# Second half's K transform in front of two rows of the first inverse, two tiles for modulation weights, spectra of block 1 kept in tiles

## The chip, the cores and the metric

The kernel runs on one core of one Trainium2 chip. The core has five engines with an instruction stream each: PE (matmuls), DVE (vector), ACT (activations), POOL and SP. Here POOL does little arithmetic and issues one queue of DMA transfers, SP issues another. The metric is the device time of one execution in microseconds, as the median of several runs. The profile shows one further execution, whose own time is given beside its span.

## The reference

The input is a sequence u of 2048 tokens with 576 channels. Six vectors sa, ca, ga, sb, cb, gb of 576 numbers come from a condition vector c. A state-space layer (S4D, 128 states per channel) is a long causal convolution along the sequence, one kernel K per channel; behind it stands a feed-forward layer (FFN).

```python
P = exp((A * dt)[:, :, None] * arange(2048))        # A, C, dt from the inputs
K = 2 * einsum("dn,dnl->dl", C, P).real             # 576 kernels of 2048 taps
y = irfft(rfft(K, 4096) * rfft(u, 4096))[:2048]     # causal convolution
A_ref(u) = y + u * D_skip

mod = (silu(c) @ w_mod).reshape(1, 6, 576)          # sa, ca, ga, sb, cb, gb
h = layernorm(x) * (1 + ca) + sa
x = x + ga * A_ref(h)
h = layernorm(x) * (1 + cb) + sb
x = x + gb * (relu(h @ w1) @ w2)                    # 576 -> 4608 -> 576
```

## The kernel before, in words

**Blocks and halves.** The sequence is worked through in 4 blocks (s = 0 to 3) of 512 tokens, held as tiles x of 128 partitions x 4 x 576. The channels are split in two halves, p = 0 and 1, of 288. A block's convolution is done by the discrete Fourier transform of 1024 points, whose larger factor is a matmul with a constant table (fcU for the input, fcK for the kernel, gc for the way back) and whose smaller factor, of 4, is a butterfly of additions on DVE. For each half: transform of u (PE, `ps_f`, then ACT copies it to a tile Z, then DVE's butterfly gives the spectrum U), transform of the SSM kernel's block (the same, giving K; for s above 0 a second spectrum, K2, made of K and the spectrum R of the block before), the product of spectra, one term for every earlier block t (Y += Ka * Ua, with temporaries T, on DVE at line 509), a butterfly giving V, and the inverse (PE, `ps_i`, line 983, four rows n2 = 0 to 3 of the result), which DVE adds to x. The spectra that later blocks need go to DRAM: Ud[t][p], Rd[t][p] and Kd[t][p], 1152 KB each, and are loaded into tiles Ua, R and Ka when a product needs them. All spectra tiles of the later blocks come from one pool, tag "S", of 6 buffers.

**The FFN.** Each block's FFN has 36 groups of 128 hidden channels. Both of its matmuls are split in a high and a low part: `w` tiles hold the weight's high part (an ACT copy, line 1255 or 1262) and the low part (DVE's subtraction, `w<-r,w`, in pieces of 640, 64 and 512 columns); xh, xl are those of the input. A group is 14 matmuls into `hps` (line 1284; 2 PSUM buffers), ACT's relu `hh` (line 1289), DVE's remainder `hl` (line 1290), which frees the `hps` buffer, and 14 matmuls into `acc` (line 1309). The low parts are made in block 0 and kept in DRAM for the later blocks.

**Interleaving.** Block 0's convolution, `conv0`, comes ahead of the first FFN and is written out by hand. The convolution of block s + 1 runs inside the FFN of block s: it is a generator (`conv(s)`) which `step` advances twice per FFN group, by an amount set by a rate per block. The SSM kernel's generation for later blocks (`kps`, line 440 on PE, lines 408 to 414 on DVE, from tables W1d, W2d and Zd in DRAM) is interleaved in the same way. A tile scheduler then fixes the order of instructions on each engine, and every engine runs its own stream in order: an instruction that waits holds up all behind it. Tiles with a tag share a fixed number of buffers, so a new tile waits for the last reader of the one whose place it takes. POOL issues its transfers in program order as well.

**The end of `conv0`.** It works with tiles of its own, tags S0 to S3, kt, and two PSUM pools (one of 2 buffers, for the first inverse, and one of 4). In the program's order it does: the first half up to V; the second half's transform of u; x's load; the first half's inverse (`back`, rows n2 = 0, 2, 1, 3, each with the addition to x and a `bn_stats` for the second norm); the second half's butterfly U1; its K transform (`transform1`, lines 786 and 788: for each of 8 results one matmul with `early` and one with `early` or the negated table `fcKn`, then an ACT copy into WK, line 789); K1, the product Y1, V1; the second half's inverse; the norm; transposes of h (`ps_t`, line 1034); the FFN's first matmul.

**The late modulation weights** (`mod_late`). sb, cb and gb are needed for the second norm and the FFN's end. For each of them POOL loads a 576 x 576 slice of w_mod in two pieces (1152 and 144 KB, lines 596 and 597) into a tile with tag "wm", of which there is one buffer; PE multiplies it with c (`mps`, line 626, 25 instructions, each recorded in two), ACT copies the row, PE transposes it (`mpt`, lines 637 and 638) and ACT writes the vector.

## Time and profile before

| | us |
|---|---|
| median of 3 runs | 1384.04 |
| lowest, highest | 1380.11, 1387.81 |
| profiled execution, its own time | 1382.06 |
| its span (first to last instruction) | 1380.3 |
| PE busy | 1233.1 |
| DVE busy | 869.9 |
| ACT busy | 503.1 |
| first matmul of the FFN starts at | 232.61 |

The mean granted clock of PE was 0.939 of full speed. A profile row reads: start, busy time, engine, line, operation, output<-inputs, shapes; in brackets the time for which the engine stood idle just before and the instruction that released it. A line number is that of the kernel before; line 509 is a helper through which most of DVE's arithmetic goes, so such rows are told apart by their tiles' names. PEclk is the clock that the throttle granted to PE in a stretch.

### The profile page before, as it was taken

How to read it: one execution, taken by the hardware profiler on the slowest of the kernel's cores; microseconds unless marked ns; L12 is line 12 of the kernel's file. 1: busy time of each engine (PE TensorE's matmuls, PEld its weight loads, DVE VectorE, ACT ScalarE, POOL GpSimd, SP SyncE). 2: the span in 40 equal slices, each digit the busy share in tenths (PEclk: the TensorE clock that was granted, in tenths of full speed). 3: DMA queues.
4: the chain of work that ended last, by engine and by line, in shares of the span. 5: the costliest groups of instructions: out<-in, count | busy, mean ns of one | idle time of the engine just before them, and what ended most of it. 6: DMA issues, size and time to landing. Idle time of an engine off the chain costs nothing.

```text
span 1380.3 us, 26042 instructions
## 1 busy us (share of the span) xinstructions
PE 1233.1 (89%) x10608; PEld 977.5 (71%) x10608; DVE 869.9 (63%) x1351; ACT 503.1 (36%) x1014; POOL 197.9 (14%) x275
## 2 busy tenths in 40 slices
PE   5124778999999987989999999999999999999998
PEld 3123556777777766667777877777877878888886
DVE  5976977999886698559834987264999232111111
ACT  7985233222224322522234324433322253222231
POOL 1776222111121100021010010000010000000000
PEclk9555787999999999899999999999999999999999
DMA  6666399788888949598788995676998657666651
GB/s 193 240 242 239 101 331 364 271 314 306 283 317 282 334 157 337 164 353 316 238 279 304 323 369 179 204 240 210 365 323 299 202 152 212 198 198 193 205 172 60
DMA packets 134568, 347.55 MB, mean 252 GB/s; under 512 B 22448, under 2 KB 22768, under 8 KB 134448
## 3 DMA queue, kind: packets, MB, share of 16 engines
q1 hardware_dynamic: 106256, 218.36, 48.6%
q0 software_dynamic: 27904, 126.94, 25.2%
q8 instruction: 83, 1.36, 0.4%
q10 hardware_dynamic: 288, 0.59, 0.1%
q14 instruction: 37, 0.30, 0.1%
HBM read 264.44 MB, written 81.40 MB: 251 GB/s over the span
## 4 chain that ended last, share of the span: by engine, by line
PE 67%; DVE 18%; DMA 7%; issue 5%; ACT 3%; POOL 1%; SPq 0%; DVEq 0%; ACTq 0%; POOLq 0%
PE acc L1309 25%; PE hps L1284 25%; PE kps L440 5%; DVE Y L509 4%; PE ps_f L749 4%; DVE T L509 4%; PE kps L262 3%; DMA Ua<-Ud 2%; PE ps_i L983 2%; DVE W L509 2%; DMA Ud<-U 1%; DVE k L133 1%; DVE hl L1290 1%; PE kps L606 1%; DMA wm_gb<-in_w_mod_dram 1%
## 5 line engine op out<-in xcount | busy, mean ns | idle before, releaser
L1309 PE MATMUL acc<-hh,w 128*128 128x512 f32 x1296 | 424.2, 401 | 6.2 <-DVE w L509 6.1
L1284 PE MATMUL hps<-xh,w 128*128 128x512 f32 x1152 | 392.0, 400 | 0.6 <-issue 0.4
L1309 PEld LDWEIGHTS acc<-hh,w 128*128 128x128 f32 x1296 | 243.0, 189 | 60.3 <-DVE w L509 7.8
L1309 PE MATMUL acc<-hl,w 128*128 128x512 f32 x720 | 278.9, 399 | 0.0
L1290 DVE SCALAR_TENSOR_TENSOR hl<-hps,hh 128x512 fp32r<-128x512 f32 x144 | 98.7, 686 | 281.5 <-ACT hh L1289 281.4
L1284 PEld LDWEIGHTS hps<-xh,w 128*128 128x128 f32 x1152 | 214.8, 188 | 47.1 <-ACT xh L1046 1.1
L1284 PE MATMUL hps<-xl,w 128*128 128x512 f32 x576 | 229.0, 397 | 0.2 <-DVE xl L1051 0.2
L1289 ACT ACTIVATE hh<-hps 128x512 fp32r<-128x512 f32 x144 | 86.0, 597 | 336.4 <-PE hps L1284 335.9
L1262 ACT ACTIVATE w<-r 128x576 fp32r<-128x576 f32 x144 | 98.7, 686 | 219.1 <-issue 172.5
L1309 PEld LDWEIGHTS acc<-hl,w 128*128 128x128 f32 x720 | 135.3, 188 | 28.3
L1284 PEld LDWEIGHTS hps<-xl,w 128*128 128x128 f32 x576 | 108.2, 188 | 24.4 <-DVE xl L1051 1.2
L1255 ACT ACTIVATE w<-r 128x640 fp32r<-128x640 f32 x142 | 104.0, 732 | 18.7 <-DMA r<-in_w_dram 18.6
L262 PE MATMUL kps<-W,W 128*32 128x16 f32 x2304 | 40.0, 218 | 78.1 <-POOL W L59 49.7
L1284 PE MATMUL hps<-xs,w 128*128 128x512 f32 x288 | 95.5, 412 | 5.4 <-DVE hl L1290 5.4
L262 PEld LDWEIGHTS kps<-W,W 128*32 128x32 f32 x2304 | 37.6, 151 | 82.7 <-POOL W L59 51.0
L440 PEld LDWEIGHTS kps<-W1r,W2r 128*32 128x32 f32 x3456 | 69.0, 146 | 31.7 <-issue 17.6
L509 DVE TENSOR_TENSOR Y<-Y,T 128x1152 f32<-128x1152 f32 x64 | 84.9, 1349 | 0.2
L440 PE MATMUL kps<-W1r,W2r 128*32 128x48 f32 (+2 forms) x3456 | 78.3, 238 | 7.3 <-DVE W1r L412 4.2
L750 ACT ACTIVATE Z<-ps_f 128x288 f32<-128x288 f32 x104 | 42.4, 408 | 64.3 <-PE ps_f L749 63.7
L1284 PEld LDWEIGHTS hps<-xs,w 128*128 128x128 f32 x288 | 52.6, 188 | 18.3 <-DVE hl L1290 7.1
L509 DVE TENSOR_TENSOR w<-r,w 128x512 fp32r<-128x512 f32 (+2 forms) x108 | 57.9, 571 | 8.7 <-ACT w L1262 8.7
L509 DVE TENSOR_TENSOR W<-Z 128x576 f32<-128x576 f32 x52 | 37.0, 751 | 28.9 <-ACT Z L750 28.9
(214 smaller groups left out, 1381.7 us busy)
## 6 DMA issues: line engine op xcount, KB each, us to landing
r<-in_w_dram SPq DMA_DIRECT2D x144, 320.0 KB, 4.4
r<-in_w_dram SPq DMA_DIRECT2D x144, 288.0 KB, 3.8
w<-L1d SPq DMA_DIRECT2D x108, 320.0 KB, 3.0
w<-L2d SPq DMA_DIRECT2D x108, 288.0 KB, 3.2
W2r<-W2d POOLq DMA_DIRECT2D x18, 1536.0 KB, 9.3
W2d<-W SPq DMA_DIRECT2D x12, 1536.0 KB, 7.8
Ua<-Ud POOLq DMA_DIRECT2D x15, 1152.0 KB, 11.1
W<-W1d POOLq DMA_DIRECT2D x18, 768.0 KB, 8.9
```

The source lines that it names most:

```text
L262: self.nc.tensor.matmul(ps[32 * dd : 32 * dd + 32, 12 * u + q, :], W2[:, r, :, ch], W1[:, u, :, r, ch], start=(r == 0), stop=(r == 1),)
L440: nc.tensor.matmul(ps[32 * dd : 32 * dd + 32, q, :], W2[:, r, :, ch], W1[:, :na, r, ch], start=(r == 0), stop=(r == 1),)
L509: return self.kept(self.nc.vector.tensor_tensor(*args, **kw))
L749: kept(nc.tensor.matmul(o, fc[:, n2, c, :], src(n2), start=True, stop=True))
L750: nc.scalar.activation(Z[:, n2, c], ps[:, :PC], AF.Copy)
L983: self.nc.tensor.matmul(ps[:, :PC], a, b, start=(i == 0), stop=(i == len(todo) - 1))
L1255: nc.scalar.activation(w[:, 0], r, AF.Copy)
L1262: nc.scalar.activation(w[:, 0:D], r2[g], AF.Copy)
L1284: nc.tensor.matmul(ps, a, x, start=(i == 0), stop=(i == 13))
L1289: nc.scalar.activation(hh, ps, AF.Relu)
L1290: nc.vector.scalar_tensor_tensor(hl, ps, 0.0, hh, op0=ALU.max, op1=ALU.subtract)
L1309: nc.tensor.matmul(acc[i], a, x, start=(f == 0 and j in (0, 3, 6, 9, 12)), stop=(f == NF - 1 and j in (2, 5, 8, 11, 13)),)
```

## The change

It has three parts.

1. **Two buffers for the modulation weights.** The loads of sb's and cb's weights are issued one behind the other; gb's is issued when sb's product has been written, into sb's tile.
2. **The order at the end of `conv0`.** U1's butterfly comes first, then rows n2 = 0 and 2 of the first inverse with their additions to x, then the whole K transform of the second half, and behind its last matmul the matmuls of rows n2 = 1 and 3. Their additions to x and their statistics are done after V1, ahead of the second inverse. For space, the vector dsk (D_skip) and the table fcKn lie in the tiles of fcU and fcK, which are filled later. The FFN's first weight conversions are issued behind the last of cb's activations instead of the K transform's last one. W1d's and Zd's stores, which the program puts behind the last weight load issued so far, stand behind gb's.
3. **Spectra kept in tiles.** In block 1 the second term of the product (t = 1) multiplies with R, which is in a tile already, instead of loading the same numbers again as Ka. In all blocks the second half's U stays in a tile (in the pool of h, which has been read by then), so that the term t = s does not load it; in the last block it isn't stored. This takes six transfers of 1152 KB away: two Ka and one Ua in block 1, one Ua each in blocks 2 and 3, one store of U in block 3.

The core of the diff:

```diff
-        for i, nm in ((3, "sb"), (4, "cb"), (5, "gb")):
-            w = cv.tile([P, 5, D], F32, tag="wm", bufs=1, name=f"wm_{nm}")
-            d = self.wm = self.mod_weights(w, slice(i * D, (i + 1) * D), nc.gpsimd)
-            if i == 3:
-                behind(d)
+        ws = {}
+
+        def load(i, nm):
+            w = ws[nm] = cv.tile([P, 5, D], F32, tag="wm", bufs=2, name=f"wm_{nm}")
+            self.wm = self.mod_weights(w, slice(i * D, (i + 1) * D), nc.gpsimd)
+            return self.wm
+
+        behind(load(3, "sb"))
+        load(4, "cb")
+        for nm in ("sb", "cb", "gb"):
             yield
+            w = ws[nm]
...
-            if nm == "gb":
+            if nm == "sb":
+                load(5, "gb")
+            elif nm == "gb":
                 yield
...
         def spec_U(p, Z):
-            U = self.spec(f"U_{s}_{p}")
+            if p:
+                U = self.hb.tile([P, 4, 2, PC], F32, tag="h", name=f"U_{s}_{p}")
+            else:
+                U = self.spec(f"U_{s}_{p}")
...
-            if s + 1 < NB or p == 1:
+            if s + 1 < NB:
                 self.save(self.Ud[s][p], U)
-            Us.append(U if p == 0 else None)
+            Us.append(U)
...
             R = self.load(self.Rd[s - 1][p], "R")
+            Rs.append(R)
...
-                Ka = Ks[p] if t == 0 else self.load(self.Kd[s - t][p], "Ka")
-                Ua = Us[p] if (t == s and Us[p] is not None) else self.load(self.Ud[t][p], "Ua")
+                if t == 0 or s == 1:
+                    Ka = (Rs if t else Ks)[p]
+                else:
+                    Ka = self.load(self.Kd[s - t][p], "Ka")
+                Ua = Us[p] if t == s else self.load(self.Ud[t][p], "Ua")
...
-        self.dsk = cva.tile([1, D], F32, name="dsk")
+        self.dsk = self.fcU[0:1].rearrange("p a b c -> p (a b c)")[:, :D]
...
+        fcKn = self.fcK.rearrange("p a b c -> p (a b) c")[:, 0:4]
...
-        half = back(0, ops(V))
-        next(half)
         U1 = S(3, "U1")
         run(self.butterfly2(W, U1, -1))
         self.save(self.Ud[0][1], U1)
-        run(half)
+        run(back(0, ops(V), (0, 2)))
         self.cps, self.nps = cpsb, 4
         WK = S(1, "WK")
         run(self.transform1(sK1, early[:, 1], fcKn, WK))
+        self.cps, self.nps = cpsa, 2
+        odd = [back(0, ops(V), (i,)) for i in (1, 3)]
+        with tc.issue_after(self.mm1.ins):
+            for h in odd:
+                next(h)
+        self.cps, self.nps = cpsb, 4
         next(mod)
...
-        with tc.issue_after(self.end1.ins):
+        with tc.issue_after(self.mact.ins):
             next(self.start)
...
+        for h in odd:
+            run(h)
```

**PE at the end of `conv0`**, from the middle of the first inverse to the product with sb's weights (`ps_i` is an inverse's row, `ps_f` a transform, `mps_sb` the product). Before:

```order
L983 MATMUL ps_i<-V_2295,gc 128x288 x6
L983 MATMUL ps_i<-V_2295,gcn 128x288 x2
L786 MATMUL ps_f<-kt,early 128x288
L983 MATMUL ps_i<-V_2295,gc 128x288 x2
L983 MATMUL ps_i<-V_2295,gcn 128x288
L983 MATMUL ps_i<-V_2295,gc 128x288 x4
L983 MATMUL ps_i<-V_2295,gcn 128x288
L788 MATMUL ps_f<-kt,early 128x288
L786 MATMUL ps_f<-kt,early 128x288
L788 MATMUL ps_f<-kt,fcKn 128x288
```

Now (the pairs L794 and L796 go on to the eighth between the last two pieces):

```order
L998 MATMUL ps_i<-V_2293,gc 128x288 x6
L998 MATMUL ps_i<-V_2293,gcn 128x288 x2
L794 MATMUL ps_f<-kt,early 128x288
L796 MATMUL ps_f<-kt,early 128x288
L794 MATMUL ps_f<-kt,early 128x288
L796 MATMUL ps_f<-kt,fcK 128x288
```

```order
L794 MATMUL ps_f<-kt,early 128x288
L796 MATMUL ps_f<-kt,fcK 128x288
L998 MATMUL ps_i<-V_2293,gc 128x288 x2
L998 MATMUL ps_i<-V_2293,gcn 128x288
L998 MATMUL ps_i<-V_2293,gc 128x288 x4
L998 MATMUL ps_i<-V_2293,gcn 128x288
L632 MATMUL mps_sb<-wm_sb,cb 32x128 x20
```

The eight matmuls of rows 1 and 3 have moved from behind the K transform's first matmul to behind its last.

**POOL's transfers in the same stretch**: weights, the second half's U and K on their way to DRAM (Ud_1, Rd_1), the kernel generator's tables (Zd, W1d). Before:

```order
L596 DMA wm_sb<-in_w_mod_dram 128x4x576
L740 DMA Ud_1_102<-U_2562 128x4x576
L596 DMA wm_cb<-in_w_mod_dram 128x4x576
L597 DMA wm_cb<-in_w_mod_dram 64x576
L1177 DMA Zd_99<-zs_1907 512x1x48
L1177 DMA Zd_100<-zs_1907 512x1x48
L1177 DMA W1d_85<-W_4_1806 128x2x768
L1177 DMA W1d_86<-W_4_1806 128x2x768
L1177 DMA W1d_87<-W_5_1869 128x2x768
L1177 DMA W1d_88<-W_5_1869 128x2x768
L740 DMA Rd_1_110<-K_2660 128x4x576
L596 DMA wm_gb<-in_w_mod_dram 128x4x576
```

Now:

```order
L596 DMA wm_sb<-in_w_mod_dram 128x4x576
L596 DMA wm_cb<-in_w_mod_dram 128x4x576
L597 DMA wm_cb<-in_w_mod_dram 64x576
L748 DMA Ud_1_102<-U_2549 128x4x576
L748 DMA Rd_1_110<-K_2657 128x4x576
L596 DMA wm_gb<-in_w_mod_dram 128x4x576
L597 DMA wm_gb<-in_w_mod_dram 64x576
L1195 DMA Zd_99<-zs_1907 512x1x48
L1195 DMA Zd_100<-zs_1907 512x1x48
L1195 DMA W1d_85<-W_4_1806 128x2x768
L1195 DMA W1d_86<-W_4_1806 128x2x768
L1195 DMA W1d_87<-W_5_1869 128x2x768
```

cb's load stands right behind sb's, and gb's ahead of Zd's and W1d's stores.

**DVE in block 1's second product**, inside the last groups of block 0's FFN (`K_1_1` and the first Ua are the term t = 0, Ka or R the term t = 1; `w` and `hl` belong to the FFN). Before:

```order
L509 TENSOR_TENSOR T<-K_1_1_5913,Ua 128x1152 x2
L509 TENSOR_TENSOR w_5995<-r_5958,w_5995 128x640
L1290 SCALAR_TENSOR_TENSOR hl<-hps,hh 128x512
L509 TENSOR_TENSOR w_6080<-r_5960,w_6080 128x64
L509 TENSOR_TENSOR w_6080<-r_5960,w_6080 128x512
L509 TENSOR_TENSOR w_6052<-r_6018,w_6052 128x640
L509 TENSOR_TENSOR Y_1_5955<-K_1_1_5913,Ua 128x4x288 x2
L509 TENSOR_TENSOR Y_1_5955<-Y_1_5955,T 128x4x288 x2
L1290 SCALAR_TENSOR_TENSOR hl<-hps,hh 128x512
L509 TENSOR_TENSOR T<-Ka,Ua 128x1152 x2
L509 TENSOR_TENSOR Y_1_5955<-Y_1_5955,T 128x4x288 x2
L509 TENSOR_TENSOR T<-Ka,Ua 128x1152 x2
```

Now:

```order
L509 TENSOR_TENSOR Y_1_5951<-K_1_1_5909,Ua 128x4x288 x2
L509 TENSOR_TENSOR T<-K_1_1_5909,Ua 128x1152 x2
L509 TENSOR_TENSOR Y_1_5951<-Y_1_5951,T 128x4x288 x2
L509 TENSOR_TENSOR T<-R,U_1_5469 128x1152
L509 TENSOR_TENSOR w_5987<-r_5954,w_5987 128x640
L509 TENSOR_TENSOR Y_1_5951<-Y_1_5951,T 128x4x288
L509 TENSOR_TENSOR T<-R,U_1_5469 128x1152
L1310 SCALAR_TENSOR_TENSOR hl<-hps,hh 128x512
L509 TENSOR_TENSOR Y_1_5951<-Y_1_5951,T 128x4x288
L509 TENSOR_TENSOR T<-R,U_1_5469 128x1152 x2
L509 TENSOR_TENSOR Y_1_5951<-Y_1_5951,T 128x4x288 x2
L509 TENSOR_TENSOR w_6072<-r_5956,w_6072 128x64
```

The term t = 1 reads R and the kept U, and the first `hl` of the FFN, which stood behind two of the product's operations, now stands behind nine.

26 lines of the change are left out of this document (12 added, 14 removed).

## The prediction

> **What bounds the kernel now.** I read the page first, then the chain of waits, then 5 us windows of the part ahead of the FFN, then single instructions of the two places that the change touches.
>
> ```profile
> PE 1233.1 (89%) x10608; PEld 977.5 (71%) x10608; DVE 869.9 (63%) x1351; ACT 503.1 (36%) x1014; POOL 197.9 (14%) x275
> ...
> PE 67%; DVE 18%; DMA 7%; issue 5%; ACT 3%; POOL 1%; SPq 0%; DVEq 0%; ACTq 0%; POOLq 0%
> ```
>
> PE is busy for 89% of the span and makes 67% of the chain that ended last, so a change that saves no PE work can gain only where PE waits: at most 1380.3 - 1233.1 = 147 us in all. The change touches two such places: the end of block 0's convolution, where the FFN cannot start yet (stage A), and the handover from block 0's FFN to block 1's (stage B). The chain through stage A (start, us, what; a DMA's time is from issue to landing):
>
> ```profile
> 179.18 7.19 DMA x<-in_x_dram
> ...
> 200.08 2.17 PE mps_sb L626 x50
> ...
> 202.53 6.90 DMA wm_cb<-in_w_mod_dram
> ...
> 209.57 3.87 PE mps_cb L626 x50
> ...
> 213.73 10.98 DMA wm_gb<-in_w_mod_dram
> ...
> 224.84 3.27 PE mps_gb L626 x50
> ```
>
> Two weight loads of 6.90 and 10.98 us stand in it, each behind the product of the tile before. But they are not alone late. PE and DVE in the same stretch (start, busy us, what, in brackets the idle time before it and its releaser):
>
> ```profile
> 182.92 0.65 PE L786 MATMUL ps_f<-kt,early 128*128 128x288 f32 x2
> ...
> 192.64 0.65 PE L788 MATMUL ps_f<-kt,early 128*128 128x288 f32 x2
> ...
> 199.43 0.65 PE L788 MATMUL ps_f<-kt,fcKn 128*128 128x288 f32 x2
> ...
> 214.12 1.17 PE L983 MATMUL ps_i<-W,gc 128*128 128x288 f32 x2
> ...
> 220.54 2.10 PE L983 MATMUL ps_i<-V,gc 128*128 128x288 f32 x8
> ...
> 232.61 0.71 PE L1284 MATMUL hps<-xs,w 128*128 128x512 f32 x2
> ```
> ```profile
> 199.59 2.90 DVE L509 TENSOR_TENSOR K<-WK 128x576 f32<-128x576 f32 x6 [5.79 <-ACT WK L789]
> ...
> 213.30 1.56 DVE L509 TENSOR_TENSOR V<-W 128x288 f32<-128x288 f32 x4
> ...
> 222.68 0.46 DVE L509 TENSOR_TENSOR x<-ps_i,x 128x288 f32<-128x288 f32 x1
> ...
> 223.24 0.41 DVE L1158 BATCH_NORM_STATS2 st<-x 128x6 f32<-128x288 f32 x1
> ```
>
> K's transform starts at 182.92, stops after its first pair of matmuls for the whole first inverse, and goes on at 192.64. DVE waits 5.79 us for its result, then runs without a gap from 199.59 to the end of V at 214.86. The second inverse ends on PE at 222.64, the last x add at 223.14, and the FFN's first matmul stands 9.93 us after that add's start. So two chains arrive together: the K chain (transform, K, product, V, second inverse), and the weights' loads.
>
> **Stage A, the K transform in front.** Nothing is added in work: the same pairs, eight odd-row matmuls, six x adds. The second pair can follow the first at 182.92 + 0.48 = 183.4 instead of 192.64; the step of a pair is (199.43 - 192.64)/14 = 0.485 us. Everything behind it on DVE moves by 9.24 us: K from 199.59 to 190.35, V's end from 214.86 to 205.6. DVE is free at 190.35: what it has to do before is U (2.88 us) and two x adds with their statistics, which wait for x's landing (179.18 + 7.19 = 186.4). What is moved behind V is two x adds and two statistics, 2 x (0.46 + 0.41) = 1.74 us, so DVE reaches the second inverse's rows at 207.4. In the old run PE gave the last row 222.64 - 214.86 = 7.8 us after V's end, which is 213.4 here, so the 1.74 us lie beside PE's work. PE itself: the transform ends at 190.7, the odd rows' eight matmuls (0.243 each) by 192.7, then it waits for wm_sb.
>
> **Stage A, the loads.** The issue of the first load on POOL, two groups of DMA issues (KB each, median us to landing), and the windows:
>
> ```profile
> 184.02 0.76 POOL L596 DMA_DIRECT2D wm_sb<-in_w_mod_dram  x1
> ```
> ```profile
> W1d<-W POOLq DMA_DIRECT2D x4, 768.0 KB, 9.1
> ...
> wm_sb<-in_w_mod_dram POOLq DMA_DIRECT2D x1, 1152.0 KB, 10.3
> ```
> ```profile
> 180.00:185.00 5.00, 3.56 (x15) 2.48 (x14) 3.42 (x6) 0.00 (x0) 2.62 (x2) 1.00 0.88 242
> 185.00:190.00 5.00, 3.03 (x8) 2.22 (x9) 3.47 (x8) 0.00 (x0) 0.00 (x0) 0.80 1.03 417
> 190.00:195.00 5.00, 5.00 (x19) 3.85 (x18) 2.81 (x7) 0.82 (x2) 0.76 (x1) 0.86 1.03 420
> 195.00:200.00 5.00, 5.00 (x21) 3.63 (x20) 0.41 (x1) 2.06 (x5) 0.00 (x0) 1.00 1.04 418
> 200.00:205.00 5.00, 2.74 (x53) 1.84 (x52) 4.97 (x8) 4.24 (x10) 2.47 (x4) 1.00 0.72 245
> 205.00:210.00 5.00, 0.43 (x9) 0.46 (x13) 4.93 (x5) 0.00 (x0) 3.20 (x6) 0.50 1.03 343
> 210.00:215.00 5.00, 4.57 (x51) 2.85 (x41) 4.80 (x9) 0.48 (x3) 2.02 (x3) 0.50 1.00 415
> 215.00:220.00 5.00, 5.00 (x14) 3.60 (x14) 1.13 (x3) 0.20 (x2) 0.02 (x1) 0.63 1.03 394
> 220.00:225.00 5.00, 2.79 (x19) 1.90 (x20) 4.17 (x19) 1.12 (x5) 1.82 (x3) 1.00 0.90 278
> ```
>
> The columns after the width are busy us of PE, weight load, DVE, ACT and POOL, then the granted clock, the DMA share and GB/s. The DMA engines are nearly full from 185 on. wm_cb is now issued right behind wm_sb, at 184.8 instead of 202.53. wm_sb lands at 184.02 + 10.3 = 194.3. wm_cb has 1.3 MB (1152 KB and a small tail): at the 417 GB/s of the whole it lands 3.2 us later (197.5), and if it takes as long as wm_sb did, at 204.6. I take 200 to 201, half the rate, since SP's weights share the engines. mps_cb (3.87 us) is then done by 205, when the second inverse can start (214.12 - 9.24 = 204.9). With the late landing it ends at 208.5, its transposes 0.7 us later, and the inverse is 4.3 us late: stage A would gain 9.24 - 4.3 = 4.9.
>
> wm_gb is issued after mps_sb, at about 197, and W1d's four copies, which stood ahead of it on POOL's queue, now stand behind it. From 180 to 225 the windows sum to 3172 x 5 = 15.9 MB, of which W1d and its small neighbour Zd are 3.3. The other 12.5 must have moved when wm_gb lands: 1.2 of them by 185, 11.3 at 417 GB/s take 27.1 us, which is 212. It is needed at 213.4, when PE has finished the second inverse. So it goes off the path, by little. Its old cost behind the inverse was 224.84 - 222.64 = 2.2 us of PE wait; part of that lies beside the norm (DVE's and ACT's scaling of h, which ps_t needs), so I count 1 of the 2.2.
>
> Above that: the second inverse, 24 matmuls from 214.12 to 222.64 = 8.5 us at the granted 0.50 to 0.63, would take 24 x 0.243 = 5.8 at full clock, 2.7 less. That needs PE busy beforehand, and it is idle between the weights' products here too. I leave it out of the sum. Stage A: 9.24 + 1 = **10.2 us**, bounds 4.9 and 9.24 + 2.2 + 2.7 = 14.1.
>
> The Trainium skill (TensorE: Matmul & The Clock Gate, Part 1) says the clock falls to half after an idle window of about 3.4 us and comes back after as long a busy one. The windows with 0.43 us of PE work at clock 0.50 agree; by the rule the mps_sb to mps_cb wait of the new order leaves the inverse on the slow clock, which is what the sum already has.
>
> What is late next: the loads of W1d's copies behind wm_gb. Their data are read back only by later loads and first used after the FFN has begun; I count nothing, and a delay there would show as POOL or DVE waits around the first generated rows.
>
> **Stage B, block 1's second product.** Removed are three loads in block 1 and one each in blocks 2 and 3, and one store, of 1152 KB each.
>
> The chain, DVE, PE and two windows there:
>
> ```profile
> 520.66 16.73 DMA Ua<-Ud
> ...
> 537.40 3.42 issue
> ```
> ```profile
> 526.28 2.63 DVE L509 TENSOR_TENSOR T<-K,Ua 128x1152 f32<-128x1152 f32 x2 [2.88 <-DMA Ua<-Ud]
> ...
> 529.56 0.69 DVE L1290 SCALAR_TENSOR_TENSOR hl<-hps,hh 128x512 fp32r<-128x512 f32 x1
> ...
> 540.81 2.63 DVE L509 TENSOR_TENSOR T<-Ka,Ua 128x1152 f32<-128x1152 f32 x2 [3.43 <-issue]
> ...
> 553.78 2.89 DVE L509 TENSOR_TENSOR V<-W 128x576 f32<-128x576 f32 x6
> ```
> ```profile
> 551.24 0.80 PE L1309 MATMUL acc<-hh,w 128*128 128x512 f32 x1 [5.42 <-DVE w L509]
> ```
> ```profile
> 540.00:550.00 10.00, 5.82 (x26) 4.50 (x24) 9.19 (x8) 3.11 (x5) 0.00 (x0) 0.99 0.82 278
> 550.00:560.00 10.00, 5.73 (x11) 3.60 (x12) 9.70 (x18) 0.00 (x0) 0.00 (x0) 0.50 0.16 44
> ```
>
> The first operand (Ua of block 0) is loaded as before, so the product starts at the same distance, 526.28. The second pair (Ka and Ua of block 1, landing late) cost DVE 3.43 us; it is now in tiles. Behind that, up to V's end at 556.67, DVE has the same instructions except about 0.8 us of weight split which moves ahead of V. So V ends 3.43 - 0.8 = 2.6 us earlier with as many hl and w behind it. But the order changes: the hl that stood at 529.56 after two multiplications now comes after nine operations of the product, 12.6 us behind its start (9 x 1.31 and one w of 0.8), at 538.9. PE, which has two buffers for hps, then waits there, up to about 5 us, and not at 551.24. It has 8.5 us of idle time in these 20 us to do that in. I take **2.5 us** of gain; bounds: +4, if the half clock of 550 to 560 goes too, and -2, if PE comes out of the earlier wait slow and has not caught up at V's end.
>
> **Stage C, blocks 2 and 3.**
>
> ```profile
> 790.00:800.00 10.00, 6.58 (x27) 5.01 (x26) 10.00 (x17) 1.32 (x3) 1.52 (x2) 0.95 0.86 300
> ```
>
> PE loses 3.4 us here, waiting for DVE, not for the loads taken away. 0, bounds -3 and +3 (that loss taken away or had once more).
>
> **Sum.** 1382.06 (the profiled execution, span 1380.3) - 10.2 - 2.5 = 1369.4. That execution is 2.0 below the median of the three runs, 1384.04, so against the median I say 1371.
>
> **Rivals.** (1) The bytes set the end. If W1d's and the stores' bytes are still served beside wm_gb, their 3.3 MB at 417 GB/s take 8 us, wm_gb lands at 219.5 to 220 instead of 212, and stage A gains only 224.84 - 219.5 = 5.3 or less; with stage B 1382.06 - 5.3 - 2.5 + 2.0 = 1376, and 1378 where stage B gives nothing. For it: only 200 to 205 and the end of the stretch have DMA shares below 1. Against it: POOL's issues stand in the order given, and W1d is behind wm_gb. The Trainium skill (DMA: Bandwidth & Descriptors, Issuing engines are not separate DMA queues) says that DMAs of all issuers run on the same 16 engines and interleave; the wm loads of 6.9 to 11 us for 1.2 MB agree, and by that rule issuing early buys only the queue's place. Chance 0.18.
>
> (2) Slower: the packing of DVE. Where nine product operations run ahead of one hl, that hl is 538.9 - 529.56 = 9.3 us late, and PE stands still once its two hps buffers are full. If the same happened at the three handovers and PE lost 9.3 at each, it would be 28 - 10.2 = 18 us slower, 1402. It decides from 10.2/3 = 3.4 us per handover on. Against it: the order shows it in block 1 only, where PE has idle time anyway. Chance 0.04.
>
> (3) Better: full clock in the second inverse, all of wm_gb's wait, 4 us in stage B: 1384 - 14.1 - 4 = 1366, and 1363 with stage C's 3. Chance 0.12.
>
> (4) The loads do nothing and the K chain is held by something not seen, such as PSUM buffers of the odd rows, which now stay full until V is done: stage A 0 to 3, time 1379 to 1384. Against it: the second inverse takes its tiles from the other pool of four. Chance 0.06.
>
> **How the numbers follow.** The forecast, 1371 with its own range 1367 to 1375, has 0.60. The range for 8 in 10 takes in (1) and (3): 1362 to 1379. About 0.5% (6.9 us) is what a measurement of this kernel tells from no change, so faster means below 1377.1, slower above 1391. Faster: the forecast, (3) and a third of (1), 0.60 + 0.12 + 0.06 = 0.78; no change: the rest of (1), (4) and a little of the small (2), 0.18; slower: 0.04.
>
> **What would show it.** The pairs of K's transform without a gap from about 183; K on DVE at 190 to 191, V's end at 205 to 206; wm_cb landed by 202, mps_cb not waiting; the FFN's first matmul at 221 to 224. In block 1's second product no idle time between the first operand's operations and the second's, the PE wait of 5 us moved from 551 to about 537 before shifting by stage A's gain. Wrong: mps_gb still released by wm_gb, K waiting for anything but WK, or a wait for hl of over 6 us at more than one handover.

## The result

| | us |
|---|---|
| before, median of 4 runs (1380.11 to 1387.81) | 1385.03 |
| changed, median of 4 runs (1364.98 to 1370.46) | 1366.89 |
| ratio of changed to before, 95% interval | 0.9886 (0.986 to 0.9911) |
| profiled execution, before and changed | 1382.06 and 1365.79 |

The change makes the kernel 1.1% faster: 16 us between the two profiled executions, 18 us between the medians. The forecast was 1371 with a range of 1362 to 1379, made against the 1384.04 of the first three runs of before: the time lies in it, 4 us better than the forecast. The sum that gave it was wrong in two of its three terms, in opposite directions, so that it fits is in part luck.

### The profile page after: what moved, and what is told of

Same layout as the page of the kernel before. It is cut to its first block, busy times and chain, and to the rows that moved or that the text cites. A ratio compares the mean times of both kernels' runs of the same rounds, so it can differ in the third digit from the quotient of the medians.

```text
span 1364.0 us, 26051 instructions
## 1 busy us (share of the span) xinstructions
PE 1230.0 (90%) x10608; PEld 975.8 (72%) x10608; DVE 871.4 (64%) x1351; ACT 503.7 (37%) x1014; POOL 193.0 (14%) x269
## 4 chain that ended last, share of the span: by engine, by line
PE 66%; DVE 16%; DMA 9%; issue 5%; ACT 2%; POOL 1%; SPq 0%; DVEq 0%; ACTq 0%; POOLq 0%
PE acc L1329 26%; PE hps L1304 26%; PE kps L440 5%; PE ps_f L757 3%; DVE T L509 3%; DVE Y L509 3%; DVE W L509 2%; PE kps L262 2%; DMA Ua<-Ud 2%; DMA Ud<-U 1%; DVE k L133 1%; DMA h<-in_x_dram 1%; DMA Ka<-Rd 1%; PE ps_i L998 1%; DMA W1d<-W 1%
## 5 line engine op out<-in xcount | busy, mean ns | idle before, releaser
L1282 ACT ACTIVATE w<-r 128x576 fp32r<-128x576 f32 x144 | 98.7, 686 | 218.4 <-issue 167.3
```

The costliest lines, as they stand in the source:

```text
L1282: nc.scalar.activation(w[:, 0:D], r2[g], AF.Copy)
```

## The profile after

The page of the changed kernel:

```profile
span 1364.0 us, 26051 instructions
PE 1230.0 (90%) x10608; PEld 975.8 (72%) x10608; DVE 871.4 (64%) x1351; ACT 503.7 (37%) x1014; POOL 193.0 (14%) x269
PE 66%; DVE 16%; DMA 9%; issue 5%; ACT 2%; POOL 1%; SPq 0%; DVEq 0%; ACTq 0%; POOLq 0%
```

PE has the same 10608 instructions. Of the 16.3 us by which the span is shorter, 13.2 are idle time of PE (147.2 before, 134.0 now) and 3.1 are busy time, at a mean granted clock of 0.952 instead of 0.939. Line numbers are now those of the changed kernel: `ps_f` of the transform 794 and 796, `ps_i` 998, `mps` 632, `hps` 1304, `hl` 1310.

**Stage A, the end of block 0's convolution.** DVE, and then PE, from K to the FFN's first matmul:

```profile
186.90 2.90 DVE L509 TENSOR_TENSOR K<-WK 128x576 f32<-128x576 f32 x6 [2.00 <-ACT WK L797]
...
196.43 1.36 DVE L509 TENSOR_TENSOR Y<-Y,T 128x1152 f32<-128x1152 f32 x1
202.46 2.76 DVE L509 TENSOR_TENSOR W<-Y 128x576 f32<-128x576 f32 x4 [4.67 <-DMA Ud<-U]
205.26 1.56 DVE L509 TENSOR_TENSOR V<-W 128x288 f32<-128x288 f32 x4
...
211.81 0.46 DVE L509 TENSOR_TENSOR x<-ps_i,x 128x288 f32<-128x288 f32 x1
```
```profile
192.69 2.22 PE L632 MATMUL mps_sb<-wm_sb,cb 128*32 128x128 f32 x50 [1.42 <-DMA wm_sb<-in_w_mod_dram]
...
197.78 0.61 PE L632 MATMUL mps_cb<-wm_cb,cb 128*32 128x128 f32 x2 [2.17 <-DMA wm_cb<-in_w_mod_dram]
...
198.56 3.85 PE L632 MATMUL mps_cb<-wm_cb,cb 128*32 128x128 f32 x48
...
203.48 5.38 PE L998 MATMUL ps_i<-W,gc 128*128 128x288 f32 x12
...
209.66 2.10 PE L998 MATMUL ps_i<-V,gc 128*128 128x288 f32 x8
211.70 2.22 PE L632 MATMUL mps_gb<-wm_gb,cb 128*32 128x128 f32 x50
...
219.62 0.73 PE L1304 MATMUL hps<-xs,w 128*128 128x512 f32 x2 [0.29 <-DVE xs L1064]
```

The K transform is in front and K starts early. But in front of W, DVE waits 4.67 us for a transfer that the prediction did not name: the store of U. POOL's issues and the time to landing of three of them:

```profile
181.14 0.77 POOL L596 DMA_DIRECT2D wm_cb<-in_w_mod_dram  x1
...
183.49 0.78 POOL L748 DMA_DIRECT2D Ud<-U  x1 [1.04 <-DVE U L509]
...
195.22 0.76 POOL L596 DMA_DIRECT2D wm_gb<-in_w_mod_dram  x1 [4.35 <-PE mps_sb L632]
```
```profile
wm_cb<-in_w_mod_dram POOLq DMA_DIRECT2D x1, 1152.0 KB, 16.5
Ud<-U POOLq DMA_DIRECT2D x1, 1152.0 KB, 18.9
...
wm_gb<-in_w_mod_dram POOLq DMA_DIRECT2D x1, 1152.0 KB, 15.5
```

U1 lies in tile S3, its store takes 18.9 us behind cb's weights, and W is written into the same S3. The same store took 10.8 us in the profile before, and 11.4 us in `orderonly` (explained below), where no load of cb's weights stands ahead of it and DVE does not wait in front of W. gb's weights land at 195.22 + 15.5 = 210.7, just before PE wants them. The clock in the same stretch (the columns are those of the prediction's windows):

```profile
195.00:200.00 5.00, 2.55 (x31) 1.84 (x34) 2.75 (x3) 0.61 (x4) 4.21 (x6) 0.77 1.02 384
200.00:205.00 5.00, 4.57 (x33) 2.76 (x27) 2.54 (x4) 1.89 (x7) 0.73 (x1) 0.50 1.03 418
205.00:210.00 5.00, 5.00 (x16) 3.64 (x15) 4.39 (x12) 0.67 (x2) 0.71 (x1) 0.70 1.06 359
```

One more wait stands behind the second inverse, on ACT:

```profile
220.42 0.63 ACT L1061 ACTIVATE xh<-xf 128x512 fp32r<-128x512 f32 x1 [1.58 <-DMA W1d<-W]
```

ACT waits 1.58 us for a store of W1d before it writes xh, the high part of the FFN's input. W1d's stores take 15.9 us to land here, 9.1 before. So the FFN's first matmul stands 88.8 us after the sequence's first transform, 9.3 earlier than before (98.1), but the first relu comes only 7.2 earlier: from that matmul to the relu it is 6.9 us instead of 4.8. Of the kernels below, `conv0only`, `after_W0`, `cblate` and `cbgb` have the same wait, 1.7 to 2.7 us; `after_again` does not have it, nor has any kernel without the whole of parts 1 and 2.

**Where the 16 us are.** To compare kernels I counted five stretches from the timeline rows of each profiled execution: up to the sequence's first transform (first `ps_f<-h,early`); from there to the first relu `hh` of the FFN (stage A); to group 30's relu (block 0's FFN); to group 54's (first handover, stage B); to group 72's (second); and from group 90's to group 100's (third). All in us; the kernels are explained below.

| kernel | first transform at | A | FFN of block 0 | 1st handover | 2nd | 3rd |
|---|---|---|---|---|---|---|
| before | 134.5 | 102.9 | 276.2 | 220.9 | 138.0 | 71.1 |
| before_again | 133.9 | 98.7 | 284.0 | 220.9 | 138.8 | 71.8 |
| orderonly | 128.6 | 101.4 | 282.7 | 221.9 | 138.1 | 70.8 |
| wmonly | 128.7 | 98.9 | 278.0 | 220.1 | 138.0 | 70.2 |
| conv0only | 128.4 | 95.7 | 285.4 | 219.6 | 139.1 | 72.7 |
| keepR | 134.4 | 101.5 | 280.4 | 221.8 | 139.7 | 72.4 |
| bufonly | 131.1 | 101.9 | 280.4 | 221.5 | 138.4 | 69.8 |
| keepU | 131.7 | 101.1 | 280.2 | 219.8 | 134.6 | 67.5 |
| changed | 130.8 | 95.7 | 279.3 | 219.2 | 134.4 | 67.9 |
| after_again | 129.3 | 94.1 | 276.8 | 218.6 | 137.6 | 68.3 |
| after_W0 | 131.7 | 94.5 | 277.0 | 219.1 | 138.9 | 68.3 |
| cblate | 134.2 | 94.8 | 275.0 | 219.4 | 134.6 | 68.7 |
| cbgb | 132.9 | 98.4 | 275.3 | 218.1 | 136.2 | 68.7 |

In the two profiles alone: 3.7 us before the first transform, 7.2 in stage A, 3.1 lost again in block 0's FFN, 1.7, 3.6 and 3.2 at the handovers. Outside these stretches nothing differs: from group 72 to 90 it is 135.2 or 135.3 us and from group 100 to the last 283.2 in all thirteen profiles.

**The handovers.** In block 1's second product, the changed kernel on DVE and PE:

```profile
518.61 2.63 DVE L509 TENSOR_TENSOR Y<-K,Ua 128x1152 f32<-128x1152 f32 x2 [2.94 <-DMA Ua<-Ud]
...
530.77 0.68 DVE L1310 SCALAR_TENSOR_TENSOR hl<-hps,hh 128x512 fp32r<-128x512 f32 x1
...
542.46 2.89 DVE L509 TENSOR_TENSOR V<-W 128x576 f32<-128x576 f32 x6
```
```profile
531.51 1.22 PE L1304 MATMUL hps<-xs,w 128*128 128x512 f32 x2 [4.96 <-DVE hl L1310]
```

From the product's start to V's end it is 545.35 - 518.61 = 26.7 us (30.4 before), and PE waits 4.96 us for the `hl` that the order had put behind nine operations.

In block 2's first product, before (DVE, then POOL), and changed (POOL, then DVE):

```profile
750.67 2.63 DVE L509 TENSOR_TENSOR T<-K,Ua 128x1152 f32<-128x1152 f32 x2 [4.27 <-DMA Ua<-Ud]
756.61 1.36 DVE L509 TENSOR_TENSOR Y<-K,Ua 128x1152 f32<-128x1152 f32 x1 [3.31 <-DMA Ud<-U]
```
```profile
731.88 0.75 POOL L740 DMA_DIRECT2D Ud<-U  x1 [9.51 <-DVE U L509]
743.53 0.76 POOL L736 DMA_DIRECT2D Ua<-Ud  x1 [10.90 <-ACT Z L750]
```
```profile
722.40 0.75 POOL L748 DMA_DIRECT2D Ud<-U  x1 [9.51 <-DVE U L509]
723.15 0.76 POOL L744 DMA_DIRECT2D Ua<-Ud  x1
```
```profile
736.97 2.63 DVE L509 TENSOR_TENSOR Y<-K,Ua 128x1152 f32<-128x1152 f32 x2
```

Before, the product's first load was issued 11.7 us behind the store of the first half's U, after a wait of 10.90; DVE then waited 4.27 us for it and 3.31 for the store of the second half's U. Now U's second half lies in h's tile, the load goes out 0.75 us behind the store, and both waits are gone: what was missing before was a free buffer in the spectra's pool, as `bufonly` below shows. These waits are in the profile of before, and the prediction had not looked there.

## The experiments

**Each half of the change.** `conv0only` is the change without its part 3 (the product and `spec_U` as before):

```diff
-                if t == 0 or s == 1:
-                    Ka = (Rs if t else Ks)[p]
-                else:
-                    Ka = self.load(self.Kd[s - t][p], "Ka")
-                Ua = Us[p] if t == s else self.load(self.Ud[t][p], "Ua")
+                Ka = Ks[p] if t == 0 else self.load(self.Kd[s - t][p], "Ka")
+                Ua = Us[p] if (t == s and Us[p] is not None) else self.load(self.Ud[t][p], "Ua")
```

> Parts 1 and 2 without part 3 (the end of block 0's convolution as changed, all spectra loaded as before). Theory A (the gain ahead of the FFN is bought by the new order, the gain at the later handovers by part 3): the first FFN group's relu 10 to 11 us earlier than before, 7 to 8 of them left at group 30, no gain at the three handovers, 7 to 9 us at the end. Rival (the gain at the handovers follows from the earlier start, not from part 3): 14 to 18 us at the end. On the 3.7 us that the changed kernel already had at its first transform of the sequence (130.83 instead of 134.51 us): if they come from an edit of conv0, they are here too; if they are the spread of PE's instruction supply between executions, this transform may start anywhere between 130 and 135.

Measured: 1374.53 us, ratio 0.9931 (0.9908 to 0.9953), so 9.6 us. Stage A is that of the changed kernel (95.7), the handovers are those of before (219.6, 139.1, 72.7). Theory A holds on where the gain is bought, the rival falls. Its figures on the way did not all hold: this profiled execution, 1379.33 us, is on the slow side of the ten, only 2.7 us better than that of before, and of its lead at the first relu 4.1 us are left at group 30, not 7 to 8. W waits 3.62 us for U's store here too, and PE, done early with cb's product, waits 1.94 us for W.

`keepU` is the kernel before with only U's second half kept:

```diff
-            U = self.spec(f"U_{s}_{p}")
+            if p:
+                U = self.hb.tile([P, 4, 2, PC], F32, tag="h", name=f"U_{s}_{p}")
+            else:
+                U = self.spec(f"U_{s}_{p}")
...
-            Us.append(U if p == 0 else None)
+            Us.append(U)
...
-                Ua = Us[p] if (t == s and Us[p] is not None) else self.load(self.Ud[t][p], "Ua")
+                Ua = Us[p] if t == s else self.load(self.Ud[t][p], "Ua")
```

> Only the second half's U kept in h's tile, in all blocks; the kernel before otherwise, so block 1 still loads Ka twice. Theory A: 0 up to group 30, about 2.5 us at the first handover (the second pair no longer waits, since one of its two loads is gone and the other stands one place further ahead in the queue), 3 to 4 us each at the second and third handover: 8 to 10 us at the end. Rival (the loads do not matter, the handovers gain by the earlier start of the FFN): 0 to 2 us. Upstream, this kernel has conv0 as before: the first transform of the sequence at 134.5 us if that time belongs to the program, elsewhere between 130 and 135 if it is spread.

Measured: 1377.12 us, ratio 0.995 (0.9924 to 0.9975), 7.0 us; 1.1, 3.4 and 3.6 us less than before at the three handovers. Theory A holds in kind, with less than expected at the first handover (2.5) and at the end (8 to 10). The third handover gains, and in this profile the second, without any change in front of the FFN.

**The place or the transfers?** `bufonly` puts U's second half into h's tile too, but stores and loads it as before:

```diff
-            U = self.spec(f"U_{s}_{p}")
+            if p:
+                U = self.hb.tile([P, 4, 2, PC], F32, tag="h", name=f"U_{s}_{p}")
+            else:
+                U = self.spec(f"U_{s}_{p}")
```

> The second half's U lies in h's tile, so it takes no buffer of the spectra's pool, but it is stored and loaded back as before: the place is freed and no transfer is saved. Theory A1 (at the second and third handover the freed buffer is what counts: the next product's first load is issued 10 us earlier and DVE's waits of 4.3 and 3.3 us for it and for U's store vanish): 3 to 4 us each at these two handovers, nothing at the first, 6 to 8 at the end. Theory A2 (the saved loads count): within 1 us of before everywhere.

Measured: 1380.93 us, ratio 0.9971 (0.9951 to 0.9992), 3 to 4 us, less than A1 and more than A2. At the second handover nothing is left (138.4), at the third 1.3 to 2 us. What happens lies between, on DVE and POOL of this kernel:

```profile
732.93 0.75 POOL L736 DMA_DIRECT2D Ua<-Ud  x1
```
```profile
746.76 2.62 DVE L509 TENSOR_TENSOR Y<-K,Ua 128x1152 f32<-128x1152 f32 x2
...
816.13 2.62 DVE L509 TENSOR_TENSOR T<-Ka,Ua 128x1152 f32<-128x1152 f32 x2 [4.78 <-DMA Ua<-Ud]
```

The place does what A1 says: the load goes out early and the first product starts without a wait; from group 54 to group 66 this kernel gains 4.8 us on before (87.9 and 92.7). In the second product it then waits 4.78 us for a load; keepU, without that Ua, waits 2.47 us there:

```profile
808.92 2.63 DVE L509 TENSOR_TENSOR T<-Ka,U 128x1152 f32<-128x1152 f32 x2 [2.47 <-DMA Ka<-Rd]
```

So the freed place gives the time: from group 54 to 66 the seven profiles with U in h's tile take 87.5 to 88.4 us and the six others 92.7 to 94.4. That the saved load is what keeps it is not shown at the second handover. From group 66 to 72 it is 45.2 to 46.0 us in those six, 50.5 in bufonly, but 46.8 to 51.4 in the six that save the load as well; the changed kernel run again waits 1.57 and 2.93 us in this second product, and after_W0, with 3.88 us there, ends at 138.9, as late as bufonly. At the third handover the six take 67.5 to 68.7 us, bufonly 69.8 and the kernels without the place 70.2 to 72.7, so there place and load both seem to count, on one profile of bufonly. In time keepU and bufonly cannot be told apart: the intervals of their ratios overlap.

**R alone.** `keepR` is the kernel before with R read in place of Ka in block 1:

```diff
-                Ka = Ks[p] if t == 0 else self.load(self.Kd[s - t][p], "Ka")
+                if t == 0 or s == 1:
+                    Ka = (Rs if t else Ks)[p]
+                else:
+                    Ka = self.load(self.Kd[s - t][p], "Ka")
```

> Only block 1's term t = 1 reads the kept R in place of Ka (two loads fewer in block 1); the kernel before otherwise. Theory A: the load of Ua for the second pair moves one place ahead in the queue and lands some 5 us earlier, DVE's wait of 3.43 us goes; 2.5 to 3 us at the first handover, nothing at the others, 2 to 3 us at the end. Rival (the order on DVE that packs nine product operations ahead of hl costs PE what the missing wait saves): within 1 us of before, or slower by up to 2.

Measured: 1387.5 us, ratio 1.0005 (0.9977 to 1.0032): no gain, the rival. DVE and PE at the first handover:

```profile
537.08 1.36 DVE L509 TENSOR_TENSOR T<-R,Ua 128x1152 f32<-128x1152 f32 x1 [1.89 <-DMA Ua<-Ud]
...
541.63 0.68 DVE L1294 SCALAR_TENSOR_TENSOR hl<-hps,hh 128x512 fp32r<-128x512 f32 x1
```
```profile
542.37 1.22 PE L1288 MATMUL hps<-xs,w 128*128 128x512 f32 x2 [6.98 <-DVE hl L1294]
```

Half of DVE's wait for the second pair stays (1.89 us instead of 3.43), and the order that packs the product ahead of `hl` makes PE wait 6.98 us. With both kept, five profiles take 218.1 to 219.4 us at the first handover, against 219.6 to 221.9 with spectra loaded as before; R alone (221.8) and U alone (219.8) lie in the range of before.

**The two edits in front of the FFN, apart.** `wmonly` is the kernel before with the two buffers and the loads' new places (and dsk and fcKn moved for their space):

```diff
-            w = cv.tile([P, 5, D], F32, tag="wm", bufs=1, name=f"wm_{nm}")
+            w = ws[nm] = cv.tile([P, 5, D], F32, tag="wm", bufs=2, name=f"wm_{nm}")
...
+        behind(load(3, "sb"))
+        load(4, "cb")
...
+            if nm == "sb":
+                load(5, "gb")
```

> Only the two buffers for the modulation weights (and the two small tiles moved for their space); the order at the end of block 0's convolution and all later blocks as before. Counted from the first transform of the sequence to the first FFN group's relu (before 102.9 us, changed 95.7). Theory A (the K chain ends as late as the loads, so each alone gains little): cb's product no longer waits, but the second inverse still waits for V: 0.9 us of the inverse's start and 0 to 2 us of gb's wait, 100 to 102. Rival (the loads were the bound): 95 to 97.

`orderonly` has the new order with one buffer. Both leave one edit of part 2 out: the FFN's first weight conversions on ACT stay where they were, behind the K transform's last copy.

```diff
+        odd = [back(0, ops(V), (i,)) for i in (1, 3)]
+        with tc.issue_after(self.mm1.ins):
+            for h in odd:
+                next(h)
...
+        for h in odd:
+            run(h)
```

> Only the new order (K transform in front, odd rows behind it, their additions after V1); one buffer for the modulation weights as before, so cb's load is issued after sb's product. Theory A (both chains together): the K chain is 9 us earlier, DVE waits for U's store as in the changed kernel, but cb's weights are issued only after sb's product, behind two stores of 1152 KB, land 7 to 16 us later and hold the inverse; gb's follow behind W1d's stores and hold the first transposes: 99 to 103 us from the first transform to the first relu (before 102.9, changed 95.7). Rival (the order alone is what counts, the weights' tiles nothing): 95 to 97.

Measured: wmonly 1376.21 us, ratio 0.9971 (0.9942 to 1.0), A 98.9; orderonly 1381.04 us, ratio 0.9996 (0.9971 to 1.0022), A 101.4. Together (conv0only) A is 95.7. Against 101.2, the mean of the five executions with the old end of `conv0`, that is 2.3 us, nothing, and 5.5 us; the five spread from 98.7 to 102.9, so the 2.3 are not shown, and 98.9 lies between the theory's 100 to 102 and the rival's 95 to 97. In orderonly the theory's 99 to 103 holds, without the wait for U's store that it expected. PE of orderonly, DVE and PE of wmonly, and ACT of wmonly:

```profile
202.75 0.47 PE L637 MATMUL mpt_sb<-ident,row_sb 128*128 128x128 f32 x1 [10.77 <-ACT row_sb L610]
...
204.55 3.86 PE L626 MATMUL mps_cb<-wm_cb,cb 128*32 128x128 f32 x50 [1.08 <-DMA wm_cb<-in_w_mod_dram]
```
```profile
193.00 2.90 DVE L509 TENSOR_TENSOR K<-WK 128x576 f32<-128x576 f32 x6 [5.12 <-ACT WK L797]
```
```profile
201.05 0.48 PE L645 MATMUL mpt_sb<-ident,row_sb 128*128 128x128 f32 x1 [5.42 <-ACT row_sb L610]
```
```profile
200.10 0.74 ACT L1258 ACTIVATE w<-r 128x640 fp32r<-128x640 f32 x1 [4.56 <-DMA r<-in_w_dram]
```

In orderonly DVE had finished V at 200.7, and PE came to the inverse at 209.1, behind cb's product, whose weights landed at 204.5: the order alone leaves the loads as the bound. In wmonly the weights were there, and DVE still waited 5.12 us for the transform; its W begins at 203.92. But both kernels meet a third wait that neither the kernel before nor the changed one has (0.74 and 0.37 us in that place): ACT does its instructions in order, sb's row stands behind an FFN weight conversion that waits for its load, and PE waits 10.77 and 5.42 us for that row. In wmonly it holds the second inverse until 207.19, later than W. So the two halves together gain what neither gains alone, but that the two chains are the only reason is not shown; moving the conversions is a part of the gain that no kernel here tried alone.

**The wait for U's store.** `after_W0` is the changed kernel with W in a tile that is free:

```diff
-        W = S(3, "W")
+        W = S(0, "W")
```

> The changed kernel, but the second inverse's butterfly result W lies in the tile S0 (the first half's V, read out by then) and not in S3, whose U is still being stored: DVE's wait of 4.67 us for U's store in front of W must be gone. Theory A (cb's product holds the inverse just as long): V ends 4 to 5 us earlier, the second inverse starts at most 1 us earlier (PE is busy with cb's product and transposes until 203.4), 94.5 to 96 us from the first transform to the first relu against 95.7; within 2 us of the changed kernel at the end. Rival (the wait for U's store is what the forecast of 10 us lost): 91 to 93, and 3 to 4 us faster at the end.

Measured: 1368.34 us, ratio 0.9919 (0.9886 to 0.9951), not faster than the changed kernel. DVE's wait is gone, and PE's rows are:

```profile
198.64 2.77 DVE L509 TENSOR_TENSOR W<-Y 128x576 f32<-128x576 f32 x4
```
```profile
196.21 0.38 PE L632 MATMUL mps_cb<-wm_cb,cb 128*32 128x128 f32 x2 [1.34 <-DMA wm_cb<-in_w_mod_dram]
...
201.58 6.09 PE L998 MATMUL ps_i<-W,gc 128*128 128x288 f32 x12
```

V ends 4.7 us earlier counted from the first transform (71.3 instead of 76.0). The inverse starts 2.8 us earlier, behind cb's product, where at most 1 was expected; cb's weights landed 14.0 us after their issue in this execution, 16.5 in the changed kernel's. The first relu comes at 94.5 (95.7 and 94.1 in two executions of the changed kernel): the inverse took 9.0 us instead of 8.3 and 7.7, and ACT's wait for W1d's store is 2.55 us. The rival's 91 to 93 falls: the store's wait had other waits beside it and behind it.

**Candidates.** `cbgb` takes cb's product behind the second inverse and gb's behind the transposes, `cblate` only cb's:

```diff
-        next(mod)
         late.close()
...
         run(back(1, lambda n2: [(g(n2, c), V1[:, n2, c]) for c in range(2)] if n2 % 2 else even(n2)))
+        next(mod)
```

> The changed kernel with W in S0, and with cb's product behind the second inverse and gb's behind the norm's transposes (a candidate for a faster version). Theory A (DVE's K chain, cb's product and the norm are then the bounds in turn): the second inverse starts when W comes, 2 to 3 us earlier than in the changed kernel, cb's product runs beside the norm: 91 to 94 us from the first transform to the first relu (95.7), 2 to 4 us faster at the end. Rival (gb's product and its ACT copies now stand in front of the first FFN group): 95 to 98, not faster.

> The changed kernel with W in S0 and cb's product behind the second inverse, gb's product where it was, ahead of the norm's transposes. Theory (the inverse was held by cb's product, and gb's product behind the transposes was what the variant with both moved paid for): the inverse ends 5 us earlier as there (75.3 instead of 80.9 us after the first transform), both products run beside the norm, the first relu comes 0 to 3 us earlier than in the changed kernel (95.7). Rival (the two products, 2.2 to 3.9 us each, then stand ahead of the transposes and take back what the inverse gained): 95 to 97.

Measured: cbgb 1372.61 us, ratio 0.9941 (0.9916 to 0.9965), A 98.4; cblate 1366.41 us, ratio 0.9873 (0.9846 to 0.99), A 94.8, beside the changed kernel's 0.9868 (0.9838 to 0.9897) in the same comparison. PE of cblate:

```profile
201.93 5.47 PE L998 MATMUL ps_i<-W,gc 128*128 128x288 f32 x12 [4.41 <-DVE W L509]
...
210.25 2.22 PE L632 MATMUL mps_cb<-wm_cb,cb 128*32 128x128 f32 x50
```

And DVE, in the norm:

```profile
214.96 0.16 DVE L820 RECIPROCAL mv<-mv 128x1 f32<-128x1 f32 x1 [3.39 <-ACT mv L813]
```

The inverse ends 4.8 us earlier (76.1 instead of 80.9 after the first transform), and most of that is lost again: the norm's square roots on ACT stand behind the copies of cb's row and vector, which wait for cb's product, and DVE waits 3.39 us for them. In cbgb stage A is 3.6 us longer than in cblate; PE waits there 2.66 us for gb's row in front of the first FFN group. cbgb's rival held, just (98.4 where 95 to 98 was expected). In cblate 94.8 lies within the theory's 0 to 3 us and just outside the rival's 95 to 97, but after_again has 94.1 with cb's product in its place, so the number does not decide; the rows show what the rival says, on ACT and not on PE. Neither kernel beats the changed one.

**The same programs again.**

> The changed kernel once more, word for word. Theory S (the time of the first transform of the sequence, 130.8 us in its profile and 134.5 in that of the kernel before, is spread between executions, not an effect of the change): it moves by 1 us or more. Rival P (it belongs to the program): 130.8 again within 0.3. The time: 1364 to 1371 us, ratio 0.986 to 0.992.

> The kernel before once more, word for word. Theory S: the first transform of the sequence starts between 128 and 134 us, not at 134.5 again. Rival P: 134.5 within 0.3. From there to the first relu 101 to 103 us in both.

Measured: the changed kernel 1366.95 us, ratio 0.9868 (0.9838 to 0.9897); the kernel before 1386.54 in one execution. The first transform moves by 1.5 us (130.8 and 129.3) and by 0.6 (134.5 and 133.9); stage A by 1.6 and by 4.2 (98.7 where 101 to 103 was expected); block 0's FFN by 2.5 and by 7.8. Rival P falls both times, but 0.6 us is a weak case for theory S. So a difference of a few us in these three stretches between two single profiles says nothing of a change, and the handovers (219.2 and 218.6, 134.4 and 137.6, 67.9 and 68.3; before 220.9 twice, 138.0 and 138.8, 71.1 and 71.8) are steadier, the second least.

## Why the prediction was right, point by point

The time was right and the sum was not. Means over executions with the same code in a stretch:

| term | forecast | measured |
|---|---|---|
| stage A | 10.2 (4.9 to 14.1) | 101.2 (five with the old code) - 95.2 (changed twice, conv0only) = 6.0 |
| stage B, first handover | 2.5 (-2 to +4) | 220.7 (five without part 3) - 218.9 (five with all of it) = 1.8 |
| stage C, second and third | 0 (-3 to +3) | 138.4 - 136.3 = 2.1 and 71.3 - 68.4 = 2.9 (five and five, as above): 5.0 |
| sum | 12.7 | 12.8 |

That the two sums agree is luck: stage A gave 4.2 us less than forecast and stage C 5.0 more. The 2.1 us of the second handover are the least certain, since 134.4 to 138.9 and 138.0 to 139.1 overlap.

**Stage A was mis-sized by 4 us.** Its first step held: K starts 9.0 us earlier counted from the first transform (65.1 and 56.1; forecast 9.24), the pairs run without a gap, cb's weights land at 181.14 + 16.5 = 197.6, where cb's product waits 2.17 us for them, and gb's do not stop PE. The next step, "everything behind it on DVE moves by 9.24 us", failed. It counted DVE's instructions and not the tile that W goes into: S3 holds U1 until its store has landed, and that store had moved behind cb's weights. V's end came 4.4 us earlier instead of 9.24. But after_W0, without that wait, has the same first relu, so this is not where the time at the end went.

In the two profiles 7.2 of the 10.2 us arrive, and two terms account for the other 3.0. First, the second inverse starts 72.65 us after the first transform, where the forecast has 204.9 - 134.5 = 70.4. Of these 2.25 us, about 0.4 are cb's weights (66.9 us where 201 - 134.5 = 66.5 was counted); cb's product took 4.6 us, with one of sb's transposes in it, at a granted clock that fell to 0.50, where 3.87 was counted; and the copy of its row and its transposes, 1.07 us (202.41 to 203.48), the forecast counted only in its bound for a late landing. The inverse itself was 0.2 us shorter. Second, the 1 us counted for gb's wait did not reach the first relu: from the last x add's start to the relu it is 14.7 us in both profiles (222.68 to 237.4 and 211.81 to 226.5). PE's wait for gb's weights is gone and the FFN's first matmul is 9.3 us earlier, but ACT's wait for W1d's store has come in its place. Of W1d's copies the prediction says "I count nothing"; it looked for a delay on POOL or DVE, and it stands on ACT. The step from 7.2 to the mean of 6.0 is spread: 102.9, the profile that the forecast started from, is the highest of its five.

Two readings of the rows were off and did no harm. The odd rows' eight matmuls are recorded in two pieces of 0.243 us each, so they take 4.0 us and not 1.9; PE still waited 1.42 us for wm_sb behind them. And in the 9.24 us for which K's transform stopped, the profile before has 3.40 us in which PE waited for DVE's addition to x (row at 186.97), not only the first inverse's matmuls.

**The clock.** The second inverse took 211.76 - 203.48 = 8.3 us, the 8.5 of before, and not the 5.8 of full clock; leaving that gain out was right. In cblate, after 4.41 us of waiting, its first 12 recorded matmuls take 5.47 us, 0.46 each, where the transform's had 0.243. The Trainium skill (TensorE: Matmul & The Clock Gate, Part 1: half clock after an idle window of about 3.4 us) fits cblate; in the changed kernel two shorter waits, 1.42 and 2.17 us with 2.22 us of sb's product and a transpose between them, were followed by 0.50 as well.

**Rival 1, the bytes**, was wrong in its price and right in its direction. gb's weights landed in time, but each 1152 KB transfer that was issued earlier took longer: cb's 16.5 us instead of 6.9, gb's 15.5 instead of 11.0, U's store 18.9 instead of 10.8. The Trainium skill (DMA: Bandwidth & Descriptors, Issuing engines are not separate DMA queues) says that transfers started by different engines run on the same 16 DMA engines and interleave. The trace agrees as far as it goes: these are all POOL's, SP's loads run beside them, and the DMA share is 1.02 to 1.06 from 195 to 210. The rival's price was taken at gb's weights; it showed at U's store and at W1d's, which no rival named.

**Stage B held.** DVE's idle time between the two pairs is gone, V's end is 3.7 us earlier after the product's start (forecast 2.6), the PE wait of 5 us stands where it was said (4.96), the gain is 1.8. Its reading of the old wait was right too: the row names "issue", but that Ua landed 20.1 us after its issue at 520.66, at 540.8, when DVE went on. That the gain needs both R and U in tiles was not foreseen: with R alone there is none.

**Rival 2, the packing of `hl`**, fell at the second and third handover, which got faster. keepR shows its mechanism at the first: 6.98 us of PE wait and no gain. Rival 3's full clock in the second inverse did not come, and rival 4 fell with K's start.

**Stage C failed as a step**: "PE loses 3.4 us here, waiting for DVE, not for the loads taken away". PE did wait for DVE, but DVE was late because it had waited 4.27 and 3.31 us some 40 us earlier for a load and a store, and those waits came from the pool's buffers. The forecast costed the loads that the change removes and did not count the buffer that it frees. bufonly shows that the buffer alone takes both waits away and gains 4.8 us over the next twelve groups; keepU shows 3.4 and 3.6 us at the two handovers without the rest of the change. How much of it lasts to the end of the second handover varies between executions (134.4 and 137.6 for the changed kernel).

**What stays open.** The measured 16 to 18 us are 3 to 5 more than the table explains. The rest lies before the first transform (131.1 to 134.5 with the old code, 128.4 to 134.2 with edits of `conv0`) and in block 0's FFN (276.2 to 284.0 in two executions of the same kernel), where single profiles spread too much to tell. conv0only measured 9.6 us, 3.6 more than stage A's 6.0, so as far as medians tell the rest comes in with parts 1 and 2. Whether the edits of `conv0`'s small tiles (dsk, fcKn) help before the first transform was not tried alone, nor was the new place of the FFN's first weight conversions, nor W1d's stores in an earlier one.

## What to carry to other kernels

When work is moved earlier, follow each tile that it writes back to its last reader, stores included: a store that is queued behind a load you have pulled ahead can become the next wait. When a tile moves to another pool, count the buffer that it frees as well as the transfer that it saves, and look for the waits which that buffer caused, often tens of microseconds before the place where PE stands still. When halves of a change are tried alone (ratios of 1.0 and 0.997 here, 0.993 together), look in each trace for waits that neither whole kernel has, before the halves' missing gain is put down to two chains that end together: here an in-order engine held a row behind a conversion that waited for its load.

## What was not expected of the hardware

The kernel generator's matmuls ahead of the first transform stand behind gaps that the profile puts down to "issue", time in which the engine waited for nothing that the profile shows. They differ from execution to execution; the last two of them, before and changed:

```profile
123.09 2.15 PE L262 MATMUL kps<-W,W 128*32 128x16 f32 x127 [3.50 <-issue]
130.10 1.70 PE L262 MATMUL kps<-W,W 128*32 128x16 f32 x99 [4.86 <-issue]
```
```profile
122.42 2.14 PE L262 MATMUL kps<-W,W 128*32 128x16 f32 x127 [2.99 <-issue]
126.42 1.70 PE L262 MATMUL kps<-W,W 128*32 128x16 f32 x99 [1.86 <-issue]
```

bufonly, whose code is that of before up to there, had 2.13 and 1.87 us in the same two places, keepR 3.50 and 4.86. What decides them, no run here shows.
